# Linear attention and a multiplicative FFN on one core: plain fp32 loads, casts on chip, nine tokens to a partition, attention in 64 × 64 quarters of TensorE

## The chip, the cores and the metric

The kernel runs on one core of one Trainium2 chip. A core has five engines with instruction streams of their own, each in order: TensorE (PE in the profile, its weight loads PEld), VectorE (DVE), ScalarE (ACT), GpSimd (POOL) and SyncE (SP, which here only issues transfers). Sixteen DMA engines move data between HBM and the on-chip memory SBUF. TensorE writes its products to PSUM, eight banks of 2 KB on each of 128 partitions; the other engines read them from there. The metric is the device time of one execution in microseconds (us). Three runs of the kernel before took 260.98, 261.24 and 262.02 us, median 261.24.

## The reference

```
phi(x) = (x if x > 0 else exp(x) - 1) + 1          # q, k, v: [8 batches, 8 heads, 576 tokens, 64]
kv  = einsum('bhsd,bhse->bhde', phi(k), v)         # 64 x 64 per batch and head
z   = sum of phi(k) over the tokens
att = einsum('bhsd,bhde->bhse', phi(q), kv) / (phi(q) . z + 1e-6)
x   = att, heads side by side                      # [4608 tokens, 512]
out = (((x @ w1) * (x @ w2)) @ w3) @ w_out         # w1, w2: 512 x 1024; w3: 1024 x 1024; w_out: 1024 x 512
```

Inputs and output are fp32. Both kernels compute in bf16 with fp32 sums, fold w3 and w_out into one matrix wf = w3 @ w_out at the start, and get z from a column of ones beside v.

## The kernel before

**Tokens.** A batch of 576 tokens is cut into 512, four to a partition (token p·4 + j in partition p, j = 0 to 3), and a remainder of 64. The remainders of two batches share one tile of 128 tokens. So there are 36 tiles of 128 tokens (nine for each pair of batches), and nine chunks of four tiles for the feed-forward.

**Loads.** `load_qkv` (L105) brings a half or a whole of q, k or v of a batch from SP's queue, in rows of 1 KB; the remainders come apart in rows of 256 bytes, from SP or POOL. The weights come from POOL's queue, whose transfers turn fp32 into bf16 on the way (`load_w12`, `load_wo`, `load_w3`, L429 to L445). Some loads are held back until another has landed (GATES, L502).

**phi** takes three steps: exp on ACT (`phi_exp`, L137), min(exp, 1) on DVE (`phi_min`, L141), and max(x + 1, that) on DVE in pieces of 256 columns (`phi_max`, L162).

**Attention.** `kv_half` (L199) multiplies phi(k) of two heads with v of two heads, 64 rows of the array at a time. The upper 64 and the lower 64 rows run side by side into two PSUM banks; ACT copies one and DVE adds the other (L203, L204). q is transposed on TensorE (`q_tr`, L309) or by a DMA transpose on SP (`qt_load`, L242). `nat_units` (L265) then makes numerator and denominator for one or two tiles, eight matmuls for a tile, and divides on DVE with three operations a tile (L271 to L275). The result is transposed to xt, on TensorE (`xt_tr`, L285) or by DMA (`xt_load`, L296). Batch 0 goes another way (`first_kvz`, `first_nd`, `first_rest`), with block-diagonal weights that give xt without that transpose.

**Feed-forward.** Step F (`f_unit`, L379) makes 128 columns of (x @ w1) · (x @ w2) for a chunk: 16 matmuls of 512 columns into two PSUM tiles, an ACT copy of the one (L376), a DVE product (L377). Eight F make a chunk. Step O (`o_unit`, L386) multiplies a tile of that with wf, eight matmuls, and ACT or DVE copies the sum out; step S stores 256 KB from SP. wf is made at the start from transposed w3 (`w3_tr`, L454, and `wf_mm`, L464).

**Order.** The string ORDER (L470) fixes the order of every step. Each letter is one step, and each engine and queue takes its instructions in the order in which the steps issue them. PSUM gives four tiles of one bank to F, O, wf and xt ("mm") and two of two banks to everything of attention and to the w3 transposes ("at").

Of the kernel before, what the change touches and what calls it, by code (L numbers as in the profile page):

```python
# [8 lines left out]
F32 = mybir.dt.float32  # L9
# [4 lines left out]
P = 128  # L14
NCH = 512


@with_exitstack
def kernel(
# [14 lines left out]
    NTOK = B * S  # L34
# [3 lines left out]
    NJ = 4  # L38
    R = S - NJ * P
    JW = H * NJ * D  # L40
    RW = (H // 2) * D
    n_chunks = NTOK // NCH

    tile_of, order = {}, []
    for b in range(0, B, 2):
        for key in [("J", b, j) for j in range(NJ)] + [("J", b + 1, j) for j in range(NJ)] + [("R", b, 0)]:
            tile_of[key] = len(order)
            order.append(key)  # L50
        tile_of["R", b + 1, 0] = tile_of["R", b, 0]
    NT = len(order)
# [3 lines left out]
    ld = ctx.enter_context(tc.tile_pool(name="ld", bufs=5))  # L56
    ldr = ctx.enter_context(tc.tile_pool(name="ldr", bufs=8))
    setup = ctx.enter_context(tc.tile_pool(name="setup", bufs=2))
    phi_p = ctx.enter_context(tc.tile_pool(name="phi", bufs=1))
    e_p = ctx.enter_context(tc.tile_pool(name="e", bufs=2))  # L60
    att = ctx.enter_context(tc.tile_pool(name="att", bufs=2))
    lr = ctx.enter_context(tc.tile_pool(name="lr", bufs=2))
    ab_p = ctx.enter_context(tc.tile_pool(name="ab", bufs=2))
    sm = ctx.enter_context(tc.tile_pool(name="sm", bufs=3))
    mm_ps = ctx.enter_context(tc.tile_pool(name="mm_ps", bufs=4, space=bass.MemoryType.PSUM))
    at_ps = ctx.enter_context(tc.tile_pool(name="at_ps", bufs=2, space=bass.MemoryType.PSUM))

# [37 lines left out]
    def load_qkv(name, src, b, part, alt=False):  # L105


        if part == 3:
            t = raw[name + "r", b] = ldr.tile([P, RW], F32, tag="ldr", name=f"{name}32r")
            for hh in range(2):  # L110
                (nc.gpsimd if alt else nc.sync).dma_start(  # L111
                    out=t[hh * R:(hh + 1) * R].rearrange("p (h d) -> p h d", d=D),
                    in_=src[b, hh * 4:(hh + 1) * 4, NJ * P:S, :].rearrange("h p d -> p h d"))
            return None
        if (name, b) not in raw:
            raw[name, b] = ld.tile([P, JW], F32, tag="ld", name=f"{name}32")
        t = raw[name, b]
        h0, h1 = ((0, 4), (4, 8), (0, 8))[part]
        W = NJ * D
        return nc.sync.dma_start(  # L120
            out=t[:, h0 * W:h1 * W].rearrange("p (h x) -> p h x", x=W),
            in_=src[b, h0:h1, 0:NJ * P, :].rearrange("h (p j) d -> p h (j d)", j=NJ))


    ph = {}

    es = {}

    def phi_exp(name, b, g):

        if g == 2:
            x, e = raw[name + "r", b], e_p.tile([P, RW], BF16, tag="er", name="er")
        else:
            x = raw[name, b][:, g * (JW // 2):(g + 1) * (JW // 2)]
            e = e_p.tile([P, JW // 2], BF16, tag="e", name="e", bufs=4)
        es[name, b, g] = x, e
        nc.scalar.activation(out=e, in_=x, func=AF.Exp)  # L137

    def phi_min(name, b, g):
        e = es[name, b, g][1]  # L140
        nc.vector.tensor_scalar_min(out=e, in0=e, scalar1=1.0)  # L141

    def phi_max(name, b, hp):

        if (name, b) not in ph:
            ph[name, b] = [None, None]
        if hp == KC:
            dr = ph[name, b][1] = phi_p.tile([P, RW], BF16, tag=name + "r", name=name + "r", bufs=3)
            todo = [(dr, *es[name, b, 2])]
        else:  # L150
            if hp == 0:
                ph[name, b][0] = phi_p.tile([P, KC, NJ, 2, D], BF16, tag=name + "j", name=name + "j")
            dj = ph[name, b][0]
            x, e = es[name, b, hp // 2]
            W = NJ * D
            todo = []
            for u in range(2):
                h = 2 * (hp % 2) + u
                todo.append((dj[:, hp, :, u, :], *(t[:, h * W:(h + 1) * W].rearrange(
                    "p (j d) -> p j d", d=D) for t in (x, e))))  # L160
        for out, x, e in todo:
            nc.vector.scalar_tensor_tensor(  # L162
                out=out, in0=x, scalar=1.0, in1=e, op0=ALU.add, op1=ALU.max)

    def copy_of(alt):
        return nc.vector.tensor_copy if alt else nc.scalar.copy

    def v_unit(b, i, alt=False):

        if i < 2:  # L170
            copy_of(alt)(  # L171
                out=vt[:, :, 4 * i:4 * i + 4, 0:D],
                in_=raw["v", b].rearrange("p (h j d) -> p j h d", h=H, j=NJ)[
                    :, :, 4 * i:4 * i + 4])
        else:
            copy_of(alt)(out=vr[:, :, 0:D], in_=raw["vr", b].rearrange("p (h d) -> p h d", d=D))


    kvs, qts, xns = {}, {}, {}

    def kv_half(b, g):


        kj, kr = ph["k", b]
        if g == 0:
            kvs[b] = att.tile([P, KC, 2, D + 1], BF16, tag="kv", name="kv")
        kvp = at_ps.tile([P, 2, 512], F32, tag="at", name="kvp")
        W = 2 * (D + 1)
        for i in range(2):
            hp = 2 * g + i  # L190
            steps = [(kj[:, hp, j].rearrange("p u d -> p (u d)"),
                      vt[:, j, 2 * hp:2 * hp + 2, :].rearrange("p h e -> p (h e)"), (0, 1))
                     for j in range(NJ)]
            steps.append((kr[:, i * P:(i + 1) * P],
                          vr[:, 2 * i:2 * i + 2, :].rearrange("p h e -> p (h e)"), (g,)))
            for n, (kk, vv, halves) in enumerate(steps):
                for r in halves:
                    rows = slice(r * R, (r + 1) * R)
                    nc.tensor.matmul(  # L199
                        kvp[:, r, i * W:(i + 1) * W], kk[rows], vv[rows],  # L200
                        start=(n == 0), stop=(n == (NJ if r == g else NJ - 1)))
        kvf = lr.tile([P, 2 * W], F32, tag="kvf", name="kvf")
        nc.scalar.copy(out=kvf, in_=kvp[:, 0, 0:2 * W])  # L203
        nc.vector.tensor_tensor(  # L204
            out=kvs[b][:, 2 * g:2 * g + 2].rearrange("p a u e -> p (a u e)"), in0=kvf,
            in1=kvp[:, 1, 0:2 * W], op=ALU.add)

    def kv_full(b, g):

        kj, kr = ph["k", b]  # L210
        if g == 0:
            kvs[b] = att.tile([P, KC, 2, D + 1], BF16, tag="kv", name="kv")
        kvp = at_ps.tile([P, 2, 512], F32, tag="at", name="kvp")
        W = 2 * (D + 1)
        rows = slice(g * R, (g + 1) * R)
        for i in range(2):
            hp = 2 * g + i
            for j in range(NJ):
                nc.tensor.matmul(kvp[:, 0, i * W:(i + 1) * W],
                                 kj[:, hp, j].rearrange("p u d -> p (u d)"),  # L220
                                 vt[:, j, 2 * hp:2 * hp + 2, :].rearrange("p h e -> p (h e)"),
                                 start=(j == 0), stop=False)
# [5 lines left out]
    def kv_copy(b, g, p, alt=False):  # L228
        copy_of(alt)(out=kvs[b][:, 2 * g:2 * g + 2].rearrange("p a u e -> p (a u e)"), in_=p)
# [401 lines left out]
```

## Time and profile before

| | |
|---|---|
| median of three runs | 261.24 us |
| span of the profiled execution, first to last instruction | 258.1 us |
| median less span | 3.1 us |
| TensorE busy | 237.4 us, 92% of the span |
| VectorE, ScalarE, GpSimd busy | 167.9, 129.0, 21.1 us |
| HBM read and written | 38.80 and 9.44 MB |
| first matmul of the feed-forward | at 43.69 us |
| last matmul ends on the chain | at 254.39 us |

The page gives busy times per engine, then the span in 40 slices (busy share in tenths), then the chain that ended last: it is followed back from the last instruction, at each step to what released it. A row of a group reads "line engine operation, written <- read, shapes, count | busy us, mean ns of one | idle before, and what ended it". A row of the timeline or of the chain begins with start and length in us. Matmuls are pipelined: the length of one in the timeline holds its way through the array, and the spacing of starts is the rate. A few matmul records are missing from the trace, so groups can show 266 where 280 ran.

### The profile page before, as it was taken

What the parts mean: (1) busy time and instruction counts of PE and PEld (TensorE: products, weight loads), DVE (VectorE), ACT (ScalarE), POOL (GpSimd) and SP (SyncE); (2) the same over time, 40 slices, a digit from 0 to 9 for tenths busy, and PEclk for the clock granted to TensorE, in tenths of its full rate; (3) what the DMA queues carried; (4) which work ended last, traced back from release to release, by engine and by line L of the source; (5) the groups of instructions that cost most, each with busy time, mean ns of one, the idle gap of its engine ahead of it and who ended that gap; (6) DMA issues with size and microseconds to landing.
All of it is one profiled execution on the core that took longest, in us unless ns stands there. A gap on an engine that the chain in (4) does not pass through costs nothing.

```text
span 258.1 us, 4507 instructions
## 1 busy us (share of the span) xinstructions
PE 237.4 (92%) x1656; PEld 116.2 (45%) x1673; DVE 167.9 (65%) x426; ACT 129.0 (50%) x205; POOL 21.1 (8%) x42
## 2 busy tenths in 40 slices
PE   1138999999999999999999999999999999999994
PEld 1124554545454454455444444444444444444442
DVE  0025787969978979997968589468866543423320
ACT  2048587858478664677353645726533203331421
POOL 8000765000101000000000000000000000000000
PEclk9999999999999999999999999999999999999999
DMA  6999999999898599939988975934980124003024
GB/s 100 200 257 378 316 229 245 208 334 307 302 291 250 87 340 215 307 104 253 211 193 245 369 160 123 248 99 131 218 220 26 34 57 124 0 37 125 3 82 163
DMA packets 70085, 48.98 MB, mean 190 GB/s; under 512 B 34416, under 2 KB 64368, under 8 KB 70064
## 3 DMA queue, kind: packets, MB, share of 16 engines
q1 hardware_dynamic: 63104, 42.54, 61.4%
q0 software_dynamic: 6816, 6.03, 14.1%
q8 instruction: 13, 0.21, 0.3%
q10 hardware_dynamic: 144, 0.13, 0.1%
q14 instruction: 8, 0.07, 0.1%
HBM read 38.80 MB, written 9.44 MB: 187 GB/s over the span
## 4 chain that ended last, share of the span: by engine, by line
PE 84%; DMA 8%; ACT 2%; SPq 1%; issue 1%; DVE 1%; DVEq 0%; POOLq 0%
PE a_ps L371 25%; PE b_ps L371 24%; PE o_ps L390 23%; DMA k<-in_k_dram 4%; DMA w3b<-in_moe_w_dram 4%; PE kvp L199 3%; PE wf_ps L464 3%; PE nd L265 3%; SPq L111 1%; PE tp L309 1%; PE w3p L454 1%; PE xtp L285 1%; PE o_ps L417 1%; DVE qj L162 1%; ACT e L137 0%
## 5 line engine op out<-in xcount | busy, mean ns | idle before, releaser
L371 PEld LDWEIGHTS <-w_sb 128*128 128x128 bf16 x576 | 54.2, 98 | 63.4 <-issue 0.5
L377 DVE TENSOR_TENSOR ab<-a_sb,b_ps 128x512 bf16<-128x512 f32 x72 | 49.0, 684 | 46.6 <-PE b_ps L371 35.4
L371 PE MATMUL a_ps<-xt,w_sb 128*128 128x512 bf16 x288 | 75.1, 380 | 0.1
L371 PE MATMUL b_ps<-xt,w_sb 128*128 128x512 bf16 x288 | 74.9, 379 | 0.0
L376 ACT COPY a_sb<-a_ps 128x512 f32<-128x512 f32 x72 | 41.9, 586 | 56.8 <-PE a_ps L371 55.6
L390 PE MATMUL o_ps<-wf_sb,ab 128*128 128x512 bf16 x266 | 63.2, 379 | 0.7
L390 PEld LDWEIGHTS <-ab 128*128 128x128 bf16 x280 | 26.7, 98 | 30.8
L393 ACT COPY o_sb<-o_ps 128x512 f32<-128x512 f32 x24 | 14.0, 583 | 30.7 <-PE o_ps L390 30.7
L162 DVE SCALAR_TENSOR_TENSOR kj<-k,e 128x256 bf16<-128x256 f32 x64 | 23.6, 417 | 0.1
L162 DVE SCALAR_TENSOR_TENSOR qj<-q,e 128x256 bf16<-128x256 f32 x64 | 23.4, 417 | 0.1
L141 DVE TENSOR_SCALAR e<-e 128x1024 bf16<-128x1024 bf16 x32 | 13.4, 420 | 14.2 <-ACT e L137 14.2
L137 ACT ACTIVATE e<-q 128x1024 bf16<-128x1024 f32 x16 | 16.7, 1058 | 9.3 <-DMA q<-in_q_dram 9.1
L454 PE MATMUL w3p<-ident,w3b 128*128 128x128 bf16 x64 | 6.1, 253 | 15.0 <-ACT w3t L455 8.0
L137 ACT ACTIVATE e<-k 128x1024 bf16<-128x1024 f32 x16 | 16.9, 1056 | 4.1 <-DMA k<-in_k_dram 2.7
L275 DVE TENSOR_TENSOR xn<-nd,r 128x512 bf16<-128x512 f32 x28 | 18.0, 686 | 0.0
L464 PE MATMUL wf_ps<-wo_sb,w3t 128*128 128x512 bf16 x61 | 16.7, 412 | 1.0 <-ACT w3t L455 0.8
L454 PEld LDWEIGHTS <-w3b 128*128 128x128 bf16 x64 | 4.9, 113 | 16.6 <-DMA w3b<-in_moe_w_dram 8.2
L393 DVE COPY o_sb<-o_ps 128x512 f32<-128x512 f32 x11 | 7.6, 688 | 6.4 <-PE o_ps L390 6.4
L171 ACT CAST vt<-v 128x1024 bf16<-128x1024 f32 x9 | 9.3, 1046 | 2.0 <-DMA v<-in_v_dram 2.0
L203 ACT COPY kvf<-kvp 128x260 f32<-128x260 f32 x14 | 5.3, 375 | 8.9 <-PE kvp L199 8.7
L464 PEld LDWEIGHTS <-w3t 128*128 128x128 bf16 x64 | 6.2, 104 | 7.8 <-issue 1.7
L199 PE MATMUL kvp<-vt,kj 64*128 64x130 bf16 x224 | 9.2, 217 | 0.0
(81 smaller groups left out, 163.5 us busy)
## 6 DMA issues: line engine op xcount, KB each, us to landing
out_dram<-o_sb SPq DMA_DIRECT2D x31, 256.0 KB, 3.2
k<-in_k_dram SPq DMA_DIRECT2D x7, 1024.0 KB, 8.6
q<-in_q_dram SPq DMA_DIRECT2D x7, 1024.0 KB, 8.2
v<-in_v_dram SPq DMA_DIRECT2D x6, 1024.0 KB, 7.4
w3b<-in_moe_w_dram POOLq DMA_DIRECT2D x8, 256.0 KB, 7.1
v<-in_v_dram SPq DMA_DIRECT2D x4, 512.0 KB, 8.5
w_sb<-in_moe_w_dram POOLq DMA_DIRECT2D x8, 256.0 KB, 11.3
out_dram<-o_sb SPq DMA_DIRECT2D x9, 128.0 KB, 2.4
```

Source lines behind the costliest of these rows:

```text
L137: nc.scalar.activation(out=e, in_=x, func=AF.Exp)
L141: nc.vector.tensor_scalar_min(out=e, in0=e, scalar1=1.0)
L162: nc.vector.scalar_tensor_tensor(out=out, in0=x, scalar=1.0, in1=e, op0=ALU.add, op1=ALU.max)
L199: nc.tensor.matmul(kvp[:, r, i * W:(i + 1) * W], kk[rows], vv[rows], start=(n == 0), stop=(n == (NJ if r == g else NJ - 1)))
L275: nc.vector.tensor_tensor(out=dst.rearrange("p (c u) e -> p u c e", u=2), in0=v4[:, :, :, 0:D], in1=r[0:n].unsqueeze(3).to_broadcast([n, 2 ...
L371: nc.tensor.matmul(ps, w[:, kc, f * P:(f + 1) * P], xt[:, 4 * c:4 * c + 4, kc, :], start=(kc == 0), stop=(kc == KC - 1))
L376: nc.scalar.copy(out=a_sb, in_=a_ps)
L377: nc.vector.tensor_mul(out=abs_[c][:, f, :], in0=a_sb, in1=b_ps)
L390: nc.tensor.matmul(o_ps, ab[:, f, m * P:(m + 1) * P], wf_sb[:, f, :], start=(f == 0), stop=(f == FC - 1))
L393: copy_of(alt)(out=o_sb, in_=o_ps)
L454: nc.tensor.transpose(tp[:, kc, :], raw["w3", i][:, kc * P:(kc + 1) * P], ident)
L464: nc.tensor.matmul(wfs[i], w3ts[i][:, kc, :], wo_sb[:, kc, :], start=(kc == 0), stop=(kc == FC - 1))
```

## The change

The kernel is rewritten in all but the feed-forward's arithmetic. Part by part:

- **Loads.** All loads are plain fp32 copies on SP's queue, into a common pool of 13 buffers of 1152 or 1024 fp32 columns. q, k and v come in halves of four heads, each row the nine tokens of one partition and one head (2304 bytes). w3 comes in rows of 4 KB, w_out of 2 KB, w1 and w2 of 1 KB. The gates are gone; a load waits for its buffer.
- **Casts.** w1, w2, w_out and w3 are cast to bf16 on ACT or DVE (CA, CB, CO, C3). w3 is then transposed on TensorE as before (T3).
- **Tokens.** Nine to a partition: token p·9 + j, p = 0 to 63, so that a batch has no remainder. A half tensor holds two groups c of two heads u in 128 partitions (u, p). A "set" is 64 tokens (one j of one batch), and a tile is two sets.
- **phi** is max(x, 0) + 1 (PT, DVE) and the minimum of that and exp(x) (PM, DVE), on 1152 columns at once. It equals phi on both sides of zero.
- **Attention in quarters.** KV makes 36 matmuls of 64 rows by 64 columns of the array for four heads; rows and columns 0 to 63 and 64 to 127 form four quarters. One copy takes both PSUM banks out. ND makes a tile with 16 matmuls in quarters, then the same three DVE operations for the one tile. Batch 0 has no way of its own any more.
- **Transposes.** q of batches 0 and 1 on TensorE (QP, nine for four heads), of the others by DMA on SP (QD). Tiles 0 to 7 of xt on TensorE (XP), all others by DMA, two tiles at a time (XD).
- **Stores** are two for a tile, 128 KB each, from POOL's queue. The last tile is split in column halves as before and stored from SP and ACT.
- **The order** of all steps is new, and nine warm-up matmuls move from before the first kv to the very start.

The core of the diff (the new side; the functions removed are those printed above):

```
+ORDER = """
+L3.0 C3.0.v LO.2 LQ.0.0 EX.q.0.0 I.0 H.9 I.1 L3.1 C3.1.v LO.1 PT.q.0.0 CO.1.v T3.0.v LO.0 L3.2
...
+ND.0 ND.1 FA.5 T3.6.a T3.7.v FB.5.a ND.2 ND.3 XP.0.v XP.1.v FA.6 EX.q.1.0 LA.1 PT.k.1.0 FB.6.a
+EX.k.1.0 XP.2.v XP.3.v LA.0 CA.0.v PT.q.1.0 LB.0 CB.0.a LQ.1.1 FA.7 FB.7.v F.0.0 PM.q.1.0 LB.1
...
+S.0.p S.1.p LV.4.0 KV.2.1.v KV.3.0.v ND.9 S.2.p F.1.7 PT.k.5.0 O.4.v EX.q.3.1 LK.4.0 ND.10 EX.k.4.0
+XD.2.0 LQ.3.0 LQ.5.1 ND.11 XD.2.1 EX.q.3.0 O.5.v O.6.a PT.q.3.0 PM.q.3.0 PM.q.3.1 PT.k.4.0 LQ.4.1
+O.7.v VC.3.1.a ND.12 S.3.p EX.k.5.1 EX.q.4.1 KV.3.1.a PT.k.5.1 PM.k.5.1 VC.4.0.v S.4.p LK.4.1
+PM.k.4.0 F.2.0 QD.3.1 F.2.1 EX.k.5.0 QD.3.0 F.2.2 F.2.3 F.2.4 ND.13 ND.14 LQ.4.0 EX.q.4.0 F.2.5
+KV.4.0.a EX.k.4.1 LV.5.0 VC.5.0.v LV.7.1 ND.15 XD.3.0 XD.3.1 PM.k.5.0 F.2.6 F.2.7 O.8.a LV.4.1 ND.16
...
+S.30.p F.8.7 O.32.v S.31.p S.32.p O.33.v S.33.p O.34.a Q.35 S.34.p
+"""
...
+    free = {"ld": deque(range(13)), "mm": deque(range(4)), "at": deque(range(2))}
+    turns = {"w3t": 3, "e": 4, "phk": 4, "phq": 4, "kv": 2, "qt": 4, "xn": 3, "xt": 4, "r": 4,
+             "ab": 2, "a_sb": 3, "o_sb": 5}
...
+    def load(key, src, cols):
+        t = raw[key] = take("ld", key, [P, HW], F32, key[0])[:, 0:cols]
+        dst = t if len(src.shape) == 2 else t.rearrange("p (a x) -> p a x", a=src.shape[1])
+        nc.sync.dma_start(out=dst, in_=src)
+
+    def head_rows(src, b, h):
+        return src[b].rearrange("h (p j) d -> (h p) (j d)", j=J).rearrange(
+            "(g p) x -> p g x", p=P)[:, 2 * h:2 * h + 2]
...
+    def s_C3(i, e):
+        t = w3bs[i] = take("a_sb", None, [P, DFF], BF16, "w3b")
+        copy_of(e)(out=t, in_=raw["w3", i])
+        give("ld", ("w3", i))
...
+    def s_PT(n, b, h, e):
+        t = phs[n, b, h] = take("ph" + n, None, [P, HW], BF16, "ph" + n)
+        nc.vector.tensor_scalar(out=by_set(n, t), in0=by_set("k", raw[n, b, h]), scalar1=0.0, scalar2=1.0,
+                                op0=ALU.max, op1=ALU.add)
...
+    def s_PM(n, b, h, e):
+        t = by_set(n, phs[n, b, h])
+        nc.vector.tensor_tensor(out=t, in0=t, in1=by_set("k", es[n, b, h]), op=ALU.min)
...
+    def s_KV(b, h, e):
...
+        for j in range(J):
+            for c in range(2):
+                for u in range(2):
+                    rows = slice(u * R, (u + 1) * R)
+                    nc.tensor.matmul(kvp[c * R:(c + 1) * R, u, 0:E], kh[rows, c, j, :],
+                                     vts[b % 2][rows, h, c, j, :], start=(j == 0), stop=(j == J - 1))
+        copy_of(e)(out=kvs[b][:, h], in_=kvp[:, :, 0:E])
...
+    def s_QD(b, h, e):
+        nc.sync.dma_start(out=q_tile(b, h), in_=phs["q", b, h], transpose=True)
...
+    def s_ND(t, e):
...
+        for h in range(2):
             for u in range(2):
...
+                for c in range(2):
+                    for g in range(2):
+                        b, j = divmod(2 * t + g, J)
+                        rows = slice(c * R, (c + 1) * R)
+                        nc.tensor.matmul(
+                            nd[g * R:(g + 1) * R, c, (2 * h + u) * E:(2 * h + u + 1) * E],
+                            qts[b, h][rows, j, u * R:(u + 1) * R], kvs[b][rows, h, u, :],
+                            start=True, stop=True)
...
+    def s_XD(c0, m, e):
+        nc.sync.dma_start(
+            out=xt_of(c0)[:, 2 * m:2 * m + 2].rearrange("p m c t -> p (m c) t"),
+            in_=xns[c0][:, 2 * m:2 * m + 2].rearrange("p m n -> p (m n)"), transpose=True)
...
+    def s_S(t, e):
+        for g in range(2):
+            {"p": nc.gpsimd, "s": nc.sync}[e].dma_start(
+                out=out_rows(t, g), in_=o_sbs[t][g * R:(g + 1) * R, :])
```

In the order string, L3, LO, LA, LB, LK, LQ and LV load w3, w_out, w1, w2, k, q and v; EX is the exp, VC the copy of v to bf16, FA and FB the two halves of a row of wf; the last letter names the engine of a copy (a, v) or the queue of a store (p, s).

More of the change, by code (lines that the diff above doesn't have):

```diff
@@ L1 @@
+from collections import deque
 from contextlib import ExitStack
@@ L125 @@
[L125 to L141, printed above, removed]
@@ L165, in copy_of @@
[L165 to L188, printed above, removed]
-        for i in range(2):
[L190 to L206, printed above, removed]
```

620 lines of the change are left out of this document (206 added, 414 removed).

## The prediction

> **What bounds the kernel now.** I read the page first: busy shares, the slices, and the chain that ended last.
>
> ```profile
> PE 237.4 (92%) x1656; PEld 116.2 (45%) x1673; DVE 167.9 (65%) x426; ACT 129.0 (50%) x205; POOL 21.1 (8%) x42
> PE   1138999999999999999999999999999999999994
> DMA  6999999999898599939988975934980124003024
> PE 84%; DMA 8%; ACT 2%; SPq 1%; issue 1%; DVE 1%; DVEq 0%; POOLq 0%
> ```
>
> TensorE (PE) is full from the fourth of 40 slices on and carries 84% of the chain; the DMA engines are full only in the first third. So two quantities set the time: when TensorE starts, and how much it has to do. Then the stretches, PE, PEld, DVE, ACT, POOL, clock, DMA share, GB/s:
>
> ```profile
> 6.00:12.00 6.00, 1.14 (x9) 0.87 (x9) 0.02 (x1) 0.00 (x0) 0.62 (x4) 1.00 1.12 194
> 18.00:24.00 6.00, 5.17 (x21) 2.24 (x20) 1.87 (x5) 3.57 (x5) 0.00 (x0) 1.00 1.10 376
> 24.00:30.00 6.00, 5.95 (x45) 3.39 (x44) 5.37 (x14) 4.79 (x7) 4.71 (x8) 1.00 1.10 363
> 43.69:254.39 210.70, 209.73 (x1479) 100.83 (x1491) 148.26 (x378) 105.70 (x174) 3.06 (x5) 1.00 0.70 179
> 100.00:110.00 10.00, 10.00 (x94) 4.78 (x92) 10.00 (x30) 5.96 (x10) 0.00 (x0) 1.00 1.16 316
> ```
>
> From 43.69 to 254.39 TensorE is busy 209.73 of 210.70 us, even where VectorE (DVE) is busy 10.00 of 10.00. The ends of that stretch, from TensorE's timeline and the chain:
>
> ```profile
> 17.70 3.62 PE L464 MATMUL wf_ps<-wo_sb,w3t 128*128 128x512 bf16 x8
> 43.69 0.38 PE L371 MATMUL a_ps<-xt,w_sb 128*128 128x512 bf16 x1
> 1.24 3.78 DMA w3b<-in_moe_w_dram
> 9.04 11.36 DMA k<-in_k_dram
> 252.63 1.76 PE o_ps L417 x16
> ```
>
> The feed-forward begins at 43.69 us, after a chain that is mostly loads (k lands 11.36 us after its issue), and the last matmul leaves 258.1 − 254.4 = 3.7 us of copy and store. I write the span as 43.7 + 210.7 + 3.7 = 258.1 us. The runs' median is 261.24, so 3.1 us lie around the span.
>
> **Step 1, the head.** All loads become plain fp32 on SP's queue. Before feed-forward unit F.0.0 stand 23 of them: 15 weight pieces of 0.524 MB and eight of 0.590 MB for batch 0 and part of batch 1, together 12.58 MB. The best stretch above moved 376 GB/s with rows of 1 KB. The first load landed 3.78 us after its issue with others beside it; without them I let the stream start at 3.1 us. The last piece, LB.0, is then there at 3.1 + 12.58/0.375 = 36.7 us, its cast takes one ACT CAST (1.05, below), and F.0.0 could start at 37.8. TensorE's own chain gives the same. The last w3 piece lands at 3.1 + 9.83/0.375 = 29.3, and behind it stand cast 1.05, transposes 0.46, five wf halves of 0.86, ND.2 and ND.3 (0.8) and four XP of 0.23, 7.5 in sum, plus about 1 for the two "at" buffers: 37.8. I take 38.0, against 43.69: −5.7. Bounds: 35.5 at 0.41 MB/us (the chain then holds it near 36.5) and 43 if DVE's order, which now also holds casts and waits for landings, adds 5.
>
> **Step 2, TensorE's work from there on.** The prices, from the chain (time, length, what) and the timeline:
>
> ```profile
> 71.78 0.45 PE tp L309 x8
> 92.78 1.73 PE o_ps L390 x8
> 119.29 1.13 PE kvp L199 x36
> 122.25 0.35 PE nd L265 x16
> 122.61 0.97 PE a_ps L371 x4
> 123.58 0.86 PE b_ps L371 x4
> 155.26 0.24 PE nd L265 x8
> 67.91 0.31 PE L265 MATMUL nd<-kv,qtr 64*64 64x65 bf16 x8
> L265 PE MATMUL nd<-kv,qtr 64*64 64x65 bf16 x56 | 2.2, 198 | 0.0
> ```
>
> 72 F units of two times 0.86, 35 O units of 1.73 and the split last tile are the same on both sides, and wf lies ahead of 43.69 in both.
> - Transposes: 80 come after 43.69 now (48 tp, 32 xtp), 34 after the change, since XD and QD go through DMA. 46 × 0.056 = −2.6.
> - Attention in 64-row halves now costs 0.24 for 8 matmuls and 0.35 for 16, so 13.75 ns each plus 0.13 to enter; the a_ps group behind it takes 0.97 where others take 0.86, so 0.11 to leave.
> - ND: now 21 groups, seven batches × (0.35 + 0.35 + 0.24) = 6.6, ndr 0.23 and some 14 exits 1.5: 8.3. After: 32 tiles left, each of 16 matmuls (twice as many) in 64 × 64 quarters: 32 × (0.24 + 16 r).
> - KV: now seven batches × 1.13 and 11 exits, 9.2. After: 14 units of 36 matmuls, half as wide: 14 × (0.24 + 36 r).
> - r, the time of one quarter matmul, no trace row has. Below: 512 columns take 0.216, so 65 take 27 ns, four at once 6.9 ns each. Above: the only 64*64 row, which uses two quarters, starts its eight (0.31 − 0.198)/7 = 16 ns apart. I take 9, about half that row, since four quarters have twice the room of its two. ND 32 × 0.38 = 12.3 (+4.0), KV 14 × 0.56 = 7.9 (−1.3). Where units stand side by side a mode change is saved, about −1.
>
> Sum: −2.6 + 4.0 − 1.3 − 1 = −0.9, from −3.1 (r 6.9) to +6.2 (r 16).
>
> **Step 3, DVE, ACT, POOL, SP: hidden, while there is room.** Prices:
>
> ```profile
> L377 DVE TENSOR_TENSOR ab<-a_sb,b_ps 128x512 bf16<-128x512 f32 x72 | 49.0, 684 | 46.6 <-PE b_ps L371 35.4 <-ACT a_sb L376 8.0 <-ACT er L137 2.2
> L162 DVE SCALAR_TENSOR_TENSOR kj<-k,e 128x256 bf16<-128x256 f32 x64 | 23.6, 417 | 0.1
> L275 DVE TENSOR_TENSOR xn<-nd,r 128x512 bf16<-128x512 f32 x28 | 18.0, 686 | 0.0
> L141 DVE TENSOR_SCALAR e<-e 128x1024 bf16<-128x1024 bf16 x32 | 13.4, 420 | 14.2 <-ACT e L137 14.2
> L171 DVE CAST vt<-v 128x1024 bf16<-128x1024 f32 x7 | 4.8, 702 | 0.0
> L171 ACT CAST vt<-v 128x1024 bf16<-128x1024 f32 x9 | 9.3, 1046 | 2.0 <-DMA v<-in_v_dram 2.0
> L137 ACT ACTIVATE e<-k 128x1024 bf16<-128x1024 f32 x16 | 16.9, 1056 | 4.1 <-DMA k<-in_k_dram 2.7 <-DVE kj L162 1.2 <-DVE qj L162 0.3
> L393 DVE COPY o_sb<-o_ps 128x512 f32<-128x512 f32 x11 | 7.6, 688 | 6.4 <-PE o_ps L390 6.4
> L111 POOL DMA_DIRECT2D v32r<-in_v_dram x4 | 2.5, 619 | 16.5 <-ACT lr L357 14.0 <-DMA w_sb<-in_moe_w_dram 2.1 <-issue 0.4
> ```
>
> - phi: now 32 exp of 1.06, 32 min of 0.42, 128 max steps of 0.417, and the remainders. After: 32 exp of 1152 (1.18), 32 PT (as the cast, 0.77) and 32 PM, a bf16 minimum of two tensors, which no row has. Bounds: 0.45 (the 0.42 row scaled) and 1.35 (one element per cycle, the slope from 417 to 684 ns over 256 columns). I take 0.9, the middle. DVE: 53 instead of 71.
> - On-chip casts: 20 of 0.70 on DVE or 1.05 on ACT, 11 and 9. DVE also gets 22 of the O copies (11 now) and 36 ND tails of about 1.02.
> - All of DVE comes to 183 (178 to 198 with PM's bounds), against 168; ACT to 117, against 129. By stage: from F.0.0 to F.1.0 DVE has 8 ab (5.5), 4 ND tails (4.1), 5 PT (3.9), 7 PM (6.3) and 13 copies and casts (8.1), 27.9 beside 25 of TensorE; from F.1.0 to F.2.0 it has 27.9 too, beside as much. Operations that follow one another overlap by 0.07 each (of about 48), so 24.5: just hidden. This is where cover ends first. The stages of chunks 2 to 8 have 7 to 25 of DVE under 16 to 30 of TensorE.
> - POOL: the w3, w_out, w1 and w2 loads and 12 r loads go, 70 stores come, 70 × 0.62 = 43 of 258, hidden; o_sb's five tiles last 5 × 1.73, longer than two issues and a landing.
>
> SP loses the 40 stores and keeps 68 loads and 26 transposes, which wait in order behind DVE results:
>
> ```profile
> L242 SPq DMA_TRANSPOSE qt<-qj x4: 1627/2907/4419, 104.7 to 190.0; - x4
> L296 SPq DMA_TRANSPOSE xt<-xn x5: 1362/1966/5036, 86.6 to 204.2; - x5
> DMA to landing us min/median/max: 2.3/4.6/7.9
> ```
>
> Each XD (eight blocks, half of these xt rows) must land before the next chunk's F. Behind the second XD of chunk 2 TensorE has O.5, O.6, O.7, ND.12 and KV.3.1, 6.2 us; of chunk 3, F.2.6, F.2.7, O.8 and two ND, 6.0. The DVE tail of 1 to 2, the issue and a landing of 4.6 need 6 to 8. I charge 1.3 at each of these two; the later chunks have 10 or more. With some small waits on landings in chunks 0 and 1: +3, between 0 and 8. If the loads behind a waiting XD came late too, ACT's exp and the O copy queued behind it would wait as well.
>
> **Step 4, the tail.** The last tile's two halves each become two stores on SP and ACT, and tile 34's stores run on POOL: +0.4 (0 to 1.5).
>
> **Sum.** 38.0 + (210.7 − 0.9 + 3) + 4.1 = 254.9 span, plus 3.1 is 258.0 us, −1.2%. Less than 0.5% (1.3 us) can't be told from no change.
>
> **A page beside two of these.** The Trainium skill, "VectorE: DVE Perf Modes", section "The perf-mode tier table", lets a bf16 tensor_tensor in SBUF run at two elements per cycle; PM would be 0.75 and DVE's sum 178, the stages lighter by 1.1 each. No row here shows such an operation.
>
> **The rivals.**
> - Faster: r stays at 6.9 and the order has no waits. 37 + 207.6 + 0.5 + 4.1 + 3.1 = 252.3. For it: TensorE's 209.73 of 210.70 in a comparable order. Against: XD's covers above. 0.19.
> - No gain: the head is held by DVE's in-order queue and the two "at" buffers, so faster loads bring nothing; F.0.0 at 42, sum 262. For it: 28.5 of DVE work must pass in 38 us, much of it waiting for landings. 0.12.
> - Slower, DVE: PM costs 1.35. The two stages then hold 31.0 each, 27.6 net, 2 over TensorE each, and waits in order double that: 258 + 6 = 264. It decides from PM = 1.0 on, where net DVE equals TensorE. 0.12.
> - Slower, loads: before F.2.0 stand 53 loads, 30.1 MB, with six transposes. At 0.375 they end at 83 plus some 8 for transposes and stores, when TensorE wants them at about 90. At 0.34, as in slices where transposes mix in (316 GB/s above), they end 8 later: 265. 0.13.
> - Slower, issue: quarter matmuls start no closer than those of the kvp row, (1.13 − 0.13)/36 = 28 ns, because it is the issue that sets that spacing and not its 130 columns. ND 32 × 0.69 + KV 14 × 1.25 = 39.6 against 20.2: 277. Against it: 16 matmuls of nd in 0.35. 0.04. The Trainium skill, "TensorE: Matmul & The Clock Gate", section "Wait — 56ns, not 53.3ns?", states such a floor of about 25 ns; the trace's 13.75 ns disagrees.
>
> **How the numbers follow.** My case has 0.40 (254 to 262; two thirds below 259.9, the rest within 0.5%). Range: 251 to 266, which leaves out the issue rival, the ends of the first and of the load rival, together under 0.2. Faster: 0.27 + 0.19 + 0.05 from the nearer half of the rivals = 0.51; same: 0.13 + 0.02 = 0.15; slower 0.34.
>
> **What would show it.** Step 1: F.0.0's first matmul at 38 and above 360 GB/s from 6 to 36 us. Step 2: KV groups of 36 in 0.5 to 0.6 and ND groups of 16 near 0.3. Step 3: PM near 0.9; idle TensorE before F.2.0 and F.3.0 released by the xt transposes, each under 2. Step 4: 4.1 after the last matmul. I am wrong if F.0.0 comes after 41, if r passes 14, or if DVE shows no idle time through F.0 and F.1.

## The result and the profile after

The changed kernel takes 264.2 us (median of ten runs, 262.9 to 267.5) against 261.2 (260.0 to 262.0) for the kernel before on the same chip: a ratio of 1.0124, 95% interval 1.0092 to 1.0155. It is slower by 1.2%, where 1.2% faster was forecast. The profiled execution took 263.0 us with a span of 260.9, so 2.1 lie around the span, and the span grew by 2.8.

The page of the kernel after (busy shares, slices, the shares of the chain), to be read against the same four lines of before:

```profile
PE 231.0 (89%) x2209; PEld 111.1 (43%) x2229; DVE 165.8 (64%) x315; ACT 111.1 (43%) x152; POOL 39.5 (15%) x78
PE   1788699999979859999978999999999999999990
DMA  7999999999997999899999911744153013410442
PE 55%; DMA 24%; DVE 12%; issue 3%; ACT 2%; SPq 1%; ACTq 0%; DVEq 0%
```

TensorE has less to do (231.0 against 237.4) and starts sooner, but there are holes in slices 12 to 22, and DMA's share of the chain went from 8% to 24%. The DMA engines are 70% full or more until slice 23. By stretches of the kernel after (us; busy PE, PEld, DVE, ACT, POOL; granted clock, DMA share, GB/s):

```profile
6.00:12.00 6.00, 4.53 (x24) 2.42 (x23) 3.00 (x5) 3.11 (x3) 0.00 (x0) 1.00 1.04 409
24.00:30.00 6.00, 3.97 (x92) 2.23 (x91) 4.95 (x11) 2.48 (x6) 0.00 (x0) 1.00 1.03 396
37.55:254.09 216.54, 204.41 (x1906) 96.35 (x1922) 141.22 (x269) 91.38 (x130) 38.17 (x70) 1.00 0.70 192
63.00:90.00 27.00, 24.31 (x320) 11.48 (x320) 22.74 (x43) 14.89 (x19) 5.13 (x8) 1.00 1.00 298
90.00:114.00 24.00, 20.36 (x201) 9.42 (x203) 16.19 (x34) 10.48 (x18) 2.81 (x4) 1.00 1.00 243
114.00:144.00 30.00, 26.38 (x309) 12.29 (x311) 20.68 (x41) 13.67 (x18) 7.23 (x14) 1.00 1.11 294
0.00:144.00 144.00, 122.29 (x1393) 60.48 (x1406) 106.74 (x206) 75.18 (x95) 19.49 (x40) 1.00 1.03 320
```

The account of the span is this. The head is 37.55 us (before 43.69): −6.1. The feed-forward stretch has 204.41 us of TensorE work (before 209.73): −5.3. In the same stretch TensorE idles 12.1 us (before 0.97): +11.2. The tail, 254.09 to 260.9, is 6.8 us (before 3.7): +3.1. So 11.4 us were gained and 14.3 given back. Of the idle time 2.7, 3.6 and 3.6 us lie in the three stretches from 63 to 144 us, where the DMA share is 1.00 or more.

A full share does not by itself mean that TensorE waits. The kernel before has much the same share over the same 144 us:

```profile
0.00:144.00 144.00, 127.43 (x970) 65.05 (x981) 107.66 (x284) 84.95 (x132) 21.10 (x42) 1.00 1.01 246
```

Its TensorE waits 0.97 us in its whole feed-forward stretch. So the share says that transfers are under way all the time, and only experiments can say whether they set the time of the kernel. The share adds up the time of every packet, and packets overlap, so it can pass 1.

TensorE's, ACT's and SP's timelines of the kernel after, mostly from 63 to 144 us (start, length; in brackets the idle time before and what ended it):

```profile
37.55 1.04 PE L342 MATMUL a_ps<-xt,w_sb 128*128 128x512 bf16 x4
75.50 1.02 PE L342 MATMUL b_ps<-xt,w_sb 128*128 128x512 bf16 x4 [1.49 <-DVE ab L349]
90.61 1.04 PE L342 MATMUL a_ps<-xt,w_sb 128*128 128x512 bf16 x4 [1.05 <-DMA xt<-xn]
96.91 1.02 PE L342 MATMUL a_ps<-xt,w_sb 128*128 128x512 bf16 x4 [2.68 <-ACT a_sb L348]
144.00 1.04 PE L342 MATMUL a_ps<-xt,w_sb 128*128 128x512 bf16 x4 [1.03 <-DMA xt<-xn]
```

```profile
95.06 1.16 ACT L227 ACTIVATE eq<-q 128x1152 bf16<-128x1152 f32 x1 [4.98 <-DMA q<-in_q_dram]
128.24 1.16 ACT L249 CAST vt<-v 128x1152 bf16<-128x1152 f32 x1 [5.51 <-DMA v<-in_v_dram]
```

```profile
86.02 1.24 SPq L324 DMA_TRANSPOSE xt<-xn  x1
87.31 0.58 SPq L149 DMA_DIRECT2D q<-in_q_dram  x1
126.63 10.81 SPq L283 DMA_TRANSPOSE qt<-phq  x2
137.49 1.53 SPq L324 DMA_TRANSPOSE xt<-xn  x1
```

The wait of 2.68 us at 96.9 reads backwards like this: TensorE wants a PSUM bank, which ACT's copy of an F unit has not emptied. The copy stands behind exp of q of batch 4, which waited 4.98 us for its load. That load went out at 87.31, behind the transpose XD.2.1. Transposes also come late: two of q held SP's queue for 10.81 us from 126.63 on, behind loads issued just ahead of them, nearly all for batches 6 and 7.

### The profile page after: what moved, and what is told of

It is laid out like the page before. It is cut to its first block, busy times and chain, and to the rows that moved or that the text cites. A ratio compares the mean times of both kernels' runs of the same rounds, so it can differ in the third digit from the quotient of the medians.

```text
span 260.9 us, 5460 instructions
## 1 busy us (share of the span) xinstructions
PE 231.0 (89%) x2209; PEld 111.1 (43%) x2229; DVE 165.8 (64%) x315; ACT 111.1 (43%) x152; POOL 39.5 (15%) x78
## 4 chain that ended last, share of the span: by engine, by line
PE 55%; DMA 24%; DVE 12%; issue 3%; ACT 2%; SPq 1%; ACTq 0%; DVEq 0%
PE b_ps L342 18%; PE a_ps L342 18%; PE o_ps L364 16%; DMA q<-in_q_dram 13%; DMA w<-in_moe_w_dram 5%; DVE ab L349 3%; DVE xn L305 3%; DMA xt<-xn 2%; DMA v<-in_v_dram 2%; DMA wo<-in_moe_w_out_dram 2%; PE nd L297 1%; DVE r L304 1%; DVE phk L239 1%; PE kvp L265 1%; DVE o_sb L371 1%
## 5 line engine op out<-in xcount | busy, mean ns | idle before, releaser
L380 POOL DMA_DIRECT2D out_dram<-o_sb x70 | 38.4, 553 | 214.3 <-DVE o_sb L371 81.2
L364 PE MATMUL o_ps<-wf_sb,ab 128*128 128x512 bf16 (+1 forms) x280 | 64.0, 373 | 1.1 <-issue 0.3
L227 ACT ACTIVATE eq<-q 128x1152 bf16<-128x1152 f32 x16 | 18.6, 1164 | 18.9 <-DMA q<-in_q_dram 18.4
L227 ACT ACTIVATE ek<-k 128x1152 bf16<-128x1152 f32 x16 | 18.6, 1166 | 6.7 <-DMA k<-in_k_dram 6.7
L249 ACT CAST vt<-v 128x1152 bf16<-128x1152 f32 x10 | 11.6, 1159 | 5.8 <-DMA v<-in_v_dram 5.8
L239 DVE TENSOR_SCALAR phq<-q 128x1152 bf16<-128x1152 f32 x16 | 12.0, 752 | 2.0 <-DMA q<-in_q_dram 2.0
L246 DVE TENSOR_TENSOR phk<-phk,ek 128x1152 bf16<-128x1152 bf16 x16 | 12.0, 754 | 1.0 <-ACT ek L227 0.7
L239 DVE TENSOR_SCALAR phk<-k 128x1152 bf16<-128x1152 f32 x16 | 12.1, 754 | 0.8 <-DMA k<-in_k_dram 0.7
L246 DVE TENSOR_TENSOR phq<-phq,eq 128x1152 bf16<-128x1152 bf16 x16 | 12.0, 754 | 0.8 <-ACT eq L227 0.3
L297 PE MATMUL nd<-kv,qt 64*64 64x65 bf16 x576 | 9.6, 194 | 2.8 <-DVE xn L305 1.0
```

What stands on the lines that cost most here:

```text
L227: nc.scalar.activation(out=t, in_=raw[n, b, h], func=AF.Exp)
L239: nc.vector.tensor_scalar(out=by_set(n, t), in0=by_set("k", raw[n, b, h]), scalar1=0.0, scalar2=1.0, op0=ALU.max, op1=ALU.add)
L246: nc.vector.tensor_tensor(out=t, in0=t, in1=by_set("k", es[n, b, h]), op=ALU.min)
L249: copy_of(e)(out=vts[b % 2][:, h, :, :, 0:D], in_=raw["v", b, h].rearrange("p (c j d) -> p c j d", c=2, j=J))
L297: nc.tensor.matmul(nd[g * R:(g + 1) * R, c, (2 * h + u) * E:(2 * h + u + 1) * E], qts[b, h][rows, j, u * R:(u + 1) * R], kvs[b][rows, h, u ...
L364: nc.tensor.matmul(o_ps, abs_[c0][:, f, m * P:(m + 1) * P], wf_sb[:, f, cols], start=(f == 0), stop=(f == FC - 1))
```

## The experiments

Theories of the waits: **W/Q**, SP's order (something needed soon stands behind something not needed yet); **H**, a special case (a transpose that waits for DVE blocks the loads behind it); **B**, transfer time (the DMA engines are full, so order only chooses who waits; D in the first expectations, where W stands for W/Q). For the tail: **A**, POOL's end.

**1. The tail.**

```
- S.31.p ... S.32.p ... S.33.p ... S.34.p
+ S.31.s ... S.32.s ... S.33.s ... S.34.s
```

> The stores of tiles 31 to 34 go from SP's queue in place of POOL's; nothing else moves. In the changed kernel the last matmul ended at 254.09 and the span at 260.9, 6.8 us later, against 3.7 before; POOL ended last, with 6.4 us of draining behind its last store. Theory A (POOL's end after a late store sets the tail): the tail falls to about 4.3, the time by 2.5 us, to 261.7. Theory B (the four column-half stores of the last tile, issued two by two on SP and ACT, set the tail): no change, or a little worse, as SP now has eight more issues of 0.55 us ahead of the last: 264 to 266.

Measured: 261.98 us, ratio 1.0028 (0.9998 to 1.0058), 2.2 us under the kernel after. In the profiled executions the tail fell from 6.8 to 5.1 us (255.1 to 260.2), where A forecast 4.3. The instructions of the program's end on POOL's queue (shortest, median and longest in ns; from when to when), kernel after, then this run:

```profile
L426 POOLq DRAIN  x3: 45/93/6397, 253.7 to 260.6; - x3
```

```profile
L426 POOLq DRAIN  x3: 45/102/5744, 246.1 to 259.9; - x3
```

The longest of the three is POOL closing its queue. In the kernel after it takes 6.4 us from 253.7 on, as the last stores go out, and ends behind all other work. With the last stores on SP it takes 5.7 us from 246.1 on and lies under TensorE's work. A holds in kind; 5.1 us of tail are still more than the 3.7 of the kernel before, and no run says what the rest is.

**2 to 4. SP's order and ACT's order.** One pair of loads exchanged; four pairs; two ACT steps moved behind F units.

```
e2a: LQ.4.1 <-> LQ.5.1
e2b: also LV.5.1 <-> LV.7.1, LQ.2.1 <-> LK.5.1, LV.2.1 <-> LQ.6.1
e3:  EX.q.4.1 behind F.2.2; VC.5.1.a behind F.3.6
```

> The loads LQ.4.1 and LQ.5.1 change places in the order. LQ.4.1 then stands ahead of the second xt transpose of chunk 2 and no longer behind it; LQ.5.1, needed some 40 us later, takes its place. Theory W (an exp on ACT waits in order for a load that SP issued late, and holds the a_sb copies behind it): the 4.98 us wait of ACT before 95.06 and the 2.68 us of idle TensorE before 96.91 go, 264.2 falls to about 261.5. Rival D (the DMA engines are full there, so that another load or transpose comes late in its place): less than 1 us is gained. Rival V (VectorE is what TensorE really waits for): the idle time stays with another releaser, no gain.

> Four pairs of loads change places, always one that was needed soon with one that was needed much later: LQ.4.1 with LQ.5.1, LV.5.1 with LV.7.1, LQ.2.1 with LK.5.1, LV.2.1 with LQ.6.1. The bytes, buffers and the rest of the order stay. Theory W: the waits of ACT on loads of 0.8, 5.0 and 5.5 us before 69.07, 95.06 and 128.24 go, and of TensorE's 12.1 us of idle time between 37.6 and 254.1 some 7 go; time about 257. Rival D: idle time stays above 9, time 262 or more. Rival V: idle stays with DVE as its releaser.

> The loads stay where they were; the two ACT steps that waited longest for a load are moved behind the a_sb copies that they held up: EX.q.4.1 from ahead of F.2.0 to behind F.2.2, VC.5.1.a from ahead of ND.18 to behind F.3.6. Theory W (it is the order within ACT that turns a late load into idle TensorE): the 2.68 us before 96.91 go, and what the 5.51 us wait cost, some 3 us; time about 259. If instead the late load itself is needed at once (TensorE waits for what is made from it), the idle time comes back a few us later with the transposes or KV as releaser, and the time stays above 263.

Measured: 262.65 (1.0059, 1.0030 to 1.0088), 266.34 (1.0230, 1.0184 to 1.0276) and 266.24 us (1.0227, 1.0185 to 1.0268). The first took the 2.68 us wait away and gained 1.5, between W's 2.7 and D's less than 1. The other two took it away as well and came out 2 us slower than the kernel after, where W forecast 5 to 7 faster. TensorE's idle time in the feed-forward stretch is 9.6, 11.8 and 13.5 us (12.1 in the kernel after). TensorE's timeline of the four exchanges, then of the ACT moves:

```profile
142.30 0.45 PE L297 MATMUL nd<-kv,qt 64*64 64x65 bf16 x31 [4.25 <-DMA qt<-phq]
144.59 1.89 PE L342 MATMUL a_ps<-xt,w_sb 128*128 128x512 bf16 x4 [1.85 <-DMA xt<-xn]
```

```profile
142.68 0.65 PE L297 MATMUL nd<-kv,qt 64*64 64x65 bf16 x31 [4.45 <-DMA qt<-phq]
145.45 1.89 PE L342 MATMUL a_ps<-xt,w_sb 128*128 128x512 bf16 x4 [2.12 <-DMA xt<-xn]
```

A wait of this kind comes back some 46 us later, now on the q transposes. Two cures by different engines end at the same place, so neither this load nor ACT's order is the limit itself.

**5 to 8. Order against transfer time.**

```
e4: e3, and QD.5.1, QD.5.0, XD.4.1 ahead of LK.7.0, LQ.7.1, LK.6.0, LQ.6.0, LV.6.1 on SP
     (QD.5.0 ahead of the last three of them only)
e5: QD.2.0 ... QD.5.1  ->  QP.2.0.a ... QP.5.1.v     (transposed on TensorE)
e6: S.0.p ... S.13.p left out
e7: e2a, the three transposes of e4, and the tail of e1
```

> Edit: the two ACT moves of the run before (EX.q.4.1 behind F.2.2, VC.5.1.a behind F.3.6), and on SP the transposes QD.5.1, QD.5.0 and XD.4.1 ahead of five loads for batches 6 and 7 that stood before them. Theory Q (order in SP's one queue): those two moves left TensorE waiting 4.45 us for a q transpose that stood behind 2.9 MB of loads nobody needed yet. With the transposes ahead of them that wait falls below 1 us, TensorE's idle time in the feed-forward stretch from about 12 to 8 us, and the time from 266.2 to 261.5 us or less. Theory B (transfer time): the DMA engines are full to 144 us (loads 97 us at 400 GB/s, 14 transposes of 2.2 us each, 22 stores of 0.5 us), so the order only chooses who waits: the wait moves to the loads of batch 6 or to another transpose, and the time stays at 264 to 267 us.

> Edit to the kernel after: q of batches 2 to 5 is transposed on TensorE (QP, nine transposes for four heads and a copy on ACT or DVE) in place of the eight DMA transposes QD, in the same places of the order. Theory B: eight DMA transposes of 2.2 us of all sixteen engines go from the stretch before 144 us, 17.6 us of transfer time; the loads come earlier, TensorE's idle time in the feed-forward stretch falls from 12 to 4 us or less. TensorE gets 72 transposes more, 5.4 us at 75 ns each as in the rows of the 36 it has. Time 264.2 - 8 + 5 = 261, less if the clock stays full. Theory Q would have the same sign, since SP's queue also loses its waits. A third theory, ACT's and DVE's own order as the cause whatever the transfers do, has idle time at 12 us or more, with the copies of 1.2 us added: 269 or more.

> Edit to the kernel after: the 28 stores of tiles 0 to 13 are left out (their part of the output is missing), all else is as it was. They run on POOL's queue, so SP's queue, its order and every engine's order are untouched; only 28 transfers of 0.5 us of the DMA engines go, 22 of them before 144 us. Theory B: 11 to 14 us of transfer time freed under saturation, so loads and transposes come that much earlier by 144 us; TensorE's idle time in the feed-forward stretch falls from 12 to 5 us or less; 264.2 to 258 us or less. Theory Q: the late transfers are late by their place in SP's queue and by what SP waits for; idle time stays above 10 us and the time at 263 to 264 us.

> Edit to the kernel after: LQ.4.1 and LQ.5.1 change places, QD.5.1, QD.5.0 and XD.4.1 go ahead of the loads for batches 6 and 7, the stores of tiles 31 to 34 go to SP's queue. The first measured -1.6 us and the last -2.3 us by themselves. Theory Q: they add up and the transposes bring another 1 us (the wait of 1.03 us for xt at 144 us goes): 259.5 us, below the kernel before. Theory B: 264.2 - 2.3 for the tail, and the rest between 0 and -1.6: 260.5 to 262.

Measured: e4 264.4 us (1.0103, 1.0064 to 1.0142); e5 264.3 (1.0112, 1.0069 to 1.0154); e6 255.1 (0.9757, 0.9725 to 0.9789); e7 266.3 (1.0163, 1.0120 to 1.0206). The feed-forward stretch and the first 144 us of e6, then of e5:

```profile
38.14:249.12 210.98, 204.10 (x1906) 96.31 (x1922) 141.06 (x269) 91.56 (x130) 21.93 (x42) 1.00 0.67 179
0.00:144.00 144.00, 128.15 (x1418) 63.10 (x1431) 110.76 (x213) 78.70 (x99) 3.26 (x12) 0.99 1.01 306
```

```profile
38.75:254.67 215.92, 207.90 (x1978) 100.64 (x1994) 143.85 (x273) 95.36 (x134) 38.53 (x70) 1.00 0.62 180
0.00:144.00 144.00, 127.78 (x1464) 65.98 (x1477) 108.43 (x206) 77.10 (x97) 19.86 (x40) 0.98 0.93 312
```

And the DMA queues (packets, MB, time of their packets as a share of 16 engines' span): the kernel after, e5, e6.

```profile
q1 hardware_dynamic: 48672, 46.15, 59.1%
q0 software_dynamic: 3360, 9.18, 13.6%
```

```profile
q1 hardware_dynamic: 39200, 43.78, 52.4%
```

```profile
q0 software_dynamic: 2016, 5.51, 9.0%
```

e6 decides for B over Q. Without 28 stores, on a queue of their own and with nothing else moved, 35.5 − 22.9 = 12.6 us of packet time go from POOL's queue (0.136 × 260.9, 0.090 × 254.0). TensorE's idle time falls from 12.1 to 6.9 us, where Q held it above 10 and B said 5 or less. The wait of 2.68 us at 96.9 shrinks to 0.32, and no wait for a transpose is left. It is not VectorE that got quicker: it is busy for 141.06 us, as in the kernel after (141.22).

The runs' medians differ by 9.1 us, the spans of the two profiled executions by 6.9: 5.2 of it idle time and 1.9 the tail (4.9 us against 6.8). The tail is POOL's closing again, which is 2.0 us shorter with 42 stores than with 70:

```profile
L425 POOLq DRAIN  x3: 45/93/4433, 248.8 to 253.7; - x3
```

Packet time is no fixed price, though. The share over 144 us is still 1.01 in e6, and over the whole run the packets of SP's queue, the same transfers as before, took 157.2 us (0.619 × 254.0) against 154.2.

In e5 the packet time of SP's queue (q1) falls from 154.2 to 137.0 us. By that the eight q transposes cost 2.15 us of all sixteen engines each, while a plain load of twice the bytes costs about 1.5 (0.59 MB at 0.396 MB/us). The share falls to 0.93 and idle time to 8.0, but B had forecast 4 or less; TensorE gets 3.5 us more work, and nothing is won. SP's queue also stood still from 66.3 to 81.2 us, waiting to issue XD.2.0; the DMA engines ran dry only at the end of that, with a share of 0.02 from 78 to 81.

e4 shortened the wait at 142 us from 4.45 to 2.36 and left 2.20 at 101. Idle time is 12.2 us where Q forecast 8, and its time lies within B's range. e7 is a miss for both theories. Its profiled execution took 263.7 us, the quickest of its six runs, the slowest 269.1, and had 12.9 us of idle time: what gained 1.5 and 2.2 alone did not add up, and why is open.

**9 to 11. Loads out of the transposes' way.**

```
e8:  loads of q, k, v of batches 2 to 7 from POOL, all stores from SP
e9:  LQ.3.0, LQ.4.1 ahead of XD.2.0; LV.4.1 <-> LV.7.1, LV.5.1 <-> LQ.7.0
e10: e9's order, e5's QP, e1's tail
```

> Edit to the kernel after: the loads of q, k and v of batches 2 to 7 go to POOL's queue, all stores to SP's, which keeps the transposes. Same bytes, same order of each engine's work. Theory H (a transpose that waits for DVE holds the loads behind it on SP; seen in the run with q on TensorE, where XD.2.0 blocked SP from 66 to 81 us with the DMA engines nearly idle): the loads no longer stand behind transposes; ACT's waits for q and v loads (18 us in all after) fall below 6, TensorE's idle time in the feed-forward stretch from 12 to 6 us or less, and the tail shrinks by 2 as in the first run: 264.2 - 6 - 2 = 256. Theory B (transfer time under full DMA engines): the loads go out earlier but the transposes and stores get the smaller share and come late instead; idle time stays at 9 us or more, time 259 to 262. A third outcome, POOL's own issue of loads is slow (0.62 us each for 34 loads, in one row of the trace of before): no more than 1 us.

> Edit to the kernel after, SP's order alone: LQ.3.0 and LQ.4.1 move ahead of XD.2.0, which waits for DVE; LQ.5.1 takes LQ.4.1's place, and LV.4.1 and LV.7.1, LV.5.1 and LQ.7.0 change places. Theory H: the loads that ACT waited for (2.99, 4.98 and 5.51 us) are issued before SP blocks, and the waits go; idle time from 12 to 7 us, 264.2 to 260. Theory B: what comes first pushes the transposes back, as in the four swaps before: idle stays at 11 us or more and the time at 263 to 266.

> Edit to the kernel after: q of batches 2 to 5 on TensorE as in the run with QP, the loads ahead of XD.2.0 and the swaps as in the run beside this one, and the stores of tiles 31 to 34 on SP. The transfer time is 17.6 us less before 144 us, and the loads do not stand behind the first blocking transpose. If lateness of loads is made by both together, this takes both away: idle time from 8.0 (the run with QP) to 5 us, 264.3 - 3 - 2.3 = 259, under the kernel before. If only one mattered it stays at the better of the two runs less 2.3 for the tail: 261 to 262. TensorE's work is 3.5 us more than in the kernel after (207.9 against 204.4).

Measured: e8 289.3 us (282.4 to 292.6); e9 266.7 (1.0217, 1.0177 to 1.0258); e10 260.0 (0.9957, 0.9940 to 0.9975). e8 is far outside all three forecasts and tells nothing on H, since it changed more than the queue. From its two timelines, TensorE and POOL:

```profile
61.88 1.89 PE L342 MATMUL a_ps<-xt,w_sb 128*128 128x512 bf16 x4 [9.13 <-DVE w_sb L182]
132.23 0.65 PE L297 MATMUL nd<-kv,qt 64*64 64x65 bf16 x31 [12.19 <-DMA qt<-phq]
```

```profile
37.52 0.84 POOL L149 DMA_DIRECT2D k<-in_k_dram  x1 [35.86 <-DVE w_sb L182]
```

From 37.52 on POOL fetched k and v of later batches as buffers came free, beside the weight pieces still queued on SP, and TensorE waited 9.13 us for the cast of a piece of w1, which had itself waited 9.62 us for its load. One queue had kept the loads in order of need.

TensorE's timeline of e9:

```profile
143.38 0.65 PE L297 MATMUL nd<-kv,qt 64*64 64x65 bf16 x31 [5.22 <-DMA qt<-phq]
```

e9 speaks against H as the cause: the loads went out ahead of the blocking transpose, the wait moved to a q transpose, and idle time is 12.2 us as before the edit. e10 takes away transfer time and orders the loads, and is the first under the kernel before, between its two forecasts (259 and 261 to 262). Its idle time of 7.6 us is above the 5 forecast and hardly below e5's 8.0: the order of the loads added little.

**12 and 13. The clock, and what is left.**

```
e12: e9, and H.22 (22 matmuls of zeros) ahead of ND.22
e13: e10, and QP.5.1 behind O.11, QP.5.0 behind O.13, QP.4.0 behind F.3.4
```

> Edit to the run with SP's order alone (266.7 us): 22 matmuls of zeros (4.75 us at 0.216) stand before ND.22, where TensorE then waited 5.22 us for a q transpose; after that wait the granted clock was 0.61 from 143 to 150 us and the groups of four matmuls took 1.89 us in place of 1.03. The zeros change no result and no other engine's work. Theory C (the wait is what takes the clock away, and the clock costs time on top of the wait): TensorE is busy through the wait, the clock stays at 1.00 there, and three groups of 1.9 become 1.0: 266.7 - 2.7 = 264, with the wait itself still there. Without C (the clock falls for another reason, or the slow groups are only late data): the 4.75 us go into the wait and change nothing, or add to it: 266 to 269.

> Edit to the run with q of batches 2 to 5 on TensorE and the loads ahead (260.0 us): QP.5.1 and QP.5.0 move two and one output tiles earlier, QP.4.0 one F unit earlier. In that run the waits left are no longer for transfers (0.32 us for xt is the only one): the two nd groups behind these transposes waited 0.70, 0.44 and 0.58 us for the copies of qt. If the waits left are these, idle time falls from 7.6 to about 6 us: 258.5. If the copies then hold up the copies of the output tiles or the transfers are the bound after all: 260 as before.

(QP.5.1 and QP.5.0 pass four and two output tiles; the expectation miscounts them.) Measured: e12 266.7 us (1.0188, 1.0135 to 1.0242); e13 258.1 (0.9875, 0.9851 to 0.9899). Windows of 1.5 us (the granted clock is the third column from the end), of e9 and then of e12:

```profile
139.50:141.00 1.50, 0.00 (x0) 0.00 (x0) 0.00 (x0) 0.00 (x0) 0.89 (x2) 1.00 1.26 173
142.50:144.00 1.50, 0.62 (x31) 0.52 (x31) 0.12 (x1) 0.00 (x0) 0.00 (x0) 0.50 1.25 291
145.50:147.00 1.50, 1.50 (x5) 0.50 (x4) 1.40 (x3) 0.23 (x1) 0.00 (x0) 0.50 1.20 298
```

```profile
142.50:144.00 1.50, 1.41 (x7) 0.49 (x5) 0.00 (x0) 0.00 (x0) 0.00 (x0) 1.00 0.95 295
145.50:147.00 1.50, 0.56 (x2) 0.21 (x3) 1.43 (x5) 0.00 (x0) 0.00 (x0) 0.91 1.09 399
147.00:148.50 1.50, 1.50 (x5) 0.61 (x4) 1.39 (x2) 0.37 (x1) 0.00 (x0) 0.50 1.09 315
```

In e9 the clock is halved from about 142 to 148.5, and groups of four matmuls take 1.9 us in place of 1.0. In e12 the zeros kept it at 1.00 through the wait, and then it fell to 0.50 all the same for some 3 us, after 2.1 us of waits for qt and xt (0.50 and 1.59) that the zeros did not cover. The time did not move, so by its own expectation the run went against C; the windows, of one execution each, say that the wait does take the clock, and that the gap left over was enough. What a clock held through both waits would give was not tried.

e13 has its feed-forward stretch and its DMA share so:

```profile
37.58:250.51 212.93, 207.44 (x1977) 100.16 (x1994) 143.53 (x273) 95.56 (x134) 34.62 (x62) 1.00 0.64 184
0.00:144.00 144.00, 131.00 (x1484) 66.99 (x1498) 111.90 (x215) 82.04 (x103) 19.80 (x40) 0.99 0.95 314
```

Idle time is 5.5 us (7.6 in e10, 12.1 in the kernel after), and three transposes moved ahead were worth 1.9 us (forecast: about 6 us idle, 258.5). The share is still 0.95, but TensorE now waits only 0.3 us for a transfer; the waits that went were for the engines' own copies of qt. This version beats both kernels, by 1.25% the one before.

## Why the prediction was wrong

**Step 1, the head: right.** 37.55 us against 38.0, with 409 and 396 GB/s against the 375 assumed. The span's error adds up like this: head −0.4, work −4.4, stalls +8.2, tail +2.7, together +6.1 over the 254.9 forecast (260.9 measured).

**Step 2, TensorE's work: right in sign, −5.3 against −0.9.** From the chain and the groups of the kernel after:

```profile
46.86 0.41 PE kvp L265 x36
L265 PE MATMUL kvp<-vt,phk 64*64 64x65 bf16 x576 | 7.3, 194 | 1.6 <-DVE xn L305 1.2
L297 PE MATMUL nd<-kv,qt 64*64 64x65 bf16 x576 | 9.6, 194 | 2.8 <-DVE xn L305 1.0
```

36 matmuls in 0.41 us are (0.41 − 0.13)/36 = 7.8 ns each (an estimate, with the 0.13 us of entry worked out in the prediction), near the lower bound of 6.9 and not at 9. ND's 32 tiles take 32/36 × 9.6 = 8.5 us, not 12.3, and KV's 14 units 14/16 × 7.3 = 6.4, not 7.9: 5.3 less than forecast, of which 4.4 arrived. The issue rival (28 ns) fell. So did, for these matmuls in quarters, the floor of about 25 ns in the Trainium skill, "TensorE: Matmul & The Clock Gate", section "Wait — 56ns, not 53.3ns?".

**Step 3, prices: high.** PM's row and DVE's total:

```profile
L246 DVE TENSOR_TENSOR phk<-phk,ek 128x1152 bf16<-128x1152 bf16 x16 | 12.0, 754 | 1.0 <-ACT ek L227 0.7
```

0.754 us against the 0.9 taken. The Trainium skill, "VectorE: DVE Perf Modes", section "The perf-mode tier table", gave the estimate of 0.75, and the trace agrees. DVE was busy 165.8 us against 183 (its overlap is not counted twice there), so the DVE rival fell. The two XD waits of 1.3 us came as 1.05 before F.2.0 and 1.03 before F.4.0, none before F.3.0.

**The step that failed is the stall term of step 3: "+3, between 0 and 8".** It was +11.2. The transfers were priced only up to F.2.0 (83 + 8 = 91 us against a need at about 90), a sum with no margin, and yet the late loads were put into a rival and a sentence ("ACT's exp and the O copy queued behind it would wait as well") at no charge. (Four transposes stand before F.2.0 in the order, not the six of that rival.) What was never summed is the transfer time of everything to 144 us. As an estimate, 38.8 MB of loads at 0.396 are 98 us, 14 transposes at 2.15 are 30, and the packets of the stores took 11 (7.9% of 144): 139 of 144 us. The measured packet time is higher, 1.03 × 144 = 148.

What the runs showed in its place is waits on late transfers. Order moved them about (9.6 to 13.5 us idle in e2a, e2b, e3, e4 and e9, which changed order alone), and less transfer time shortened them (6.9 and 8.0 us in e6 and e5). Why the kernel before has no such waits with a share of 1.01 is argued and not shown. One reason may be that a head 6.1 us sooner and 5.3 us less work make TensorE want its data sooner; that 11.2 us of idle time give almost exactly these 11.4 back is partly chance, since some of the work was saved behind 144 us. Another may be the pace of the loads: the kernel after has issued its last load at 139.1 us and has a share of 0.47 from 144 to 200, while the kernel before, with its gates, issues its last load of v at 175.8. So part of the 139 us was not needed by 144, and no run held those loads back until then.

The rival "slower, loads" (265 us, 0.13) had this mechanism; with 298, 243 and 294 GB/s in the three stretches the kernel measured 264.2. None of the three signs of being wrong that the prediction named came, as none was for this term.

**Step 4, the tail: "+0.4 (0 to 1.5)" was +3.1.** The stores' move to POOL was counted as 43 us of hidden issue, and the end of POOL's queue was not looked at. Run 1 took 1.7 us of the tail away, and 2.2 of the time.

**Around the span** the prediction put 3.1 us, which mixed some 2.1 us around every span with the 1 us by which before's profiled execution (258.1 + 2.1) was quicker than its median. The kernel after's was quicker than its median by 1.2, with a granted clock of 0.997; the ten runs go from 262.9 us at 0.997 to 267.5 at 0.972.

## What to carry to other kernels

Where the DMA engines are full, sum all transfer time (loads, transposes, stores) up to the moment of need before booking a gain on the engine that waits for it: an earlier start or less work upstream may only turn into a wait. Ask too which of these transfers could come later. Here order on a queue mostly chose who waits; taking transfers away (a transpose on an engine with room, priced in the DMA engines' own time) is what shortens it, and only afterwards do small moves of engine steps pay. Put the last stores on a queue that closes quickly.

## What the runs showed of the hardware

- A wait of TensorE can cost clock on top of itself, and not every time. The same wait of 2.7 us (2.68 and 2.66) at 96 us, first in the kernel after, then in e1:

```profile
97.50:99.00 1.50, 1.50 (x9) 0.69 (x7) 0.76 (x3) 1.39 (x2) 0.00 (x0) 1.00 1.15 203
```

```profile
97.50:99.00 1.50, 1.50 (x5) 0.60 (x4) 0.47 (x1) 1.11 (x2) 0.00 (x0) 0.50 1.16 210
```

Nine matmuls against five in the same 1.5 us. The Trainium skill, "TensorE: Matmul & The Clock Gate", section "What's actually happening", puts the slow state at half clock after an idle window of about 3.4 us. The half clock agrees (0.50, for 3 to 6.5 us); the length does not, since a wait of 2.66 us was enough here. The section also says that this window runs freely. Whether that explains why one execution of two falls, and the spread of the runs from 262.9 to 267.5 us, is not shown.
- A DMA transpose of 0.29 MB took about 2.15 us of packet time of all sixteen DMA engines (e5 against the kernel after; e10 and e13 against e1 give 2.2 and 2.0), about three times the time per byte of a plain load.
- Quarter matmuls of 65 columns follow one another in about 7.8 ns (36 in 0.41 us).
- In these runs POOL's queue took longer to close the more stores it had issued: 6.4, 5.7 and 4.4 us with 70, 62 and 42 (the kernel after, e1, e6). In the kernel before, which stored nothing from POOL, it took 3.8 us, far ahead of the end.
